# Attention of the first two sequences ahead of the layers, and each layer for both of them on one conversion of its weights

## The chip, the cores and the metric

The kernel runs on one core of one Trainium2 chip. The metric is the device time of one execution in microseconds (us). Three executions of the kernel before took 1094.45, 1095.03 and 1097.45 us; their median is 1095.03 us. About 0.3% (3.3 us) is what a comparison of runs of this kernel can tell from no change.

## The reference

Four sequences of 576 tokens go through attention with 8 heads of 64 channels, and then through two feed-forward layers (512 to 2048 to 512) with different activations. Scores further than `tau` below the row's largest one are left out of the softmax.

```python
scores = scale * np.matmul(q, k.transpose(0, 1, 3, 2))          # 4 x 8 x 576 x 576
thresh = np.max(scores, axis=-1, keepdims=True) - tau
scores = np.where(scores >= thresh, scores, -1000000000.0)
attn = softmax(scores);  x = (attn @ v), heads side by side      # 2304 x 512
h = x @ w_in;  g = h * np.clip(h + 3.0, 0.0, 6.0) / 6.0;  x = g @ w_out       # layer 1
h = x @ w_in2; r = np.maximum(h, 0.0); g = r * r;         out = g @ w_out2    # layer 2
```

The activations are float32, the four weight matrices float64.

## The kernel before, in words

**Attention.** A sequence is four units, each a pair of heads. A unit is nine jobs: four blocks of 128 queries of each head, and one job for the last 64 queries of both heads; a sequence is 36 jobs. A job computes its scores (L302 or L306) into one of three PSUM slots (tag `s`), takes their minimum on VectorE (L312; the queries carry a minus sign), the threshold (L314 on GpSimd or L316 on ScalarE), the exponential on ScalarE (L322), masks and sums on VectorE (L329, which is what gives the PSUM slot back), makes float16 and a remainder (`p16`: L335 on ScalarE, L336 and L337 on GpSimd), transposes them by a DMA (L339, tile `pt`), and five jobs later multiplies by the values (L361, tile `o`). `finish` transposes a unit's result back (`xT`) and copies it to `xr` (L392). The first sequence is "plain": one float32 product per half row, with the queries in the buffer of `ya` and `p16` in the weights' buffers `wpo`. The others split queries and keys into two parts, with four times as many products, each shorter, and with more work ahead of each unit (L230 to L244).

**Layers.** A hidden tile is 24 matmuls of 288 columns (L696, tile `hp`) for 128 of the 2048 hidden channels of one sequence, then ScalarE, VectorE, ScalarE and GpSimd (L700 to L707) make its two float16 parts. An output tile is 24 matmuls (L733, tile `y`), added to `ya` by L739. Both take PSUM slots of the same tag `s` as the scores. A layer of one sequence is 16 hidden and 16 output tiles, 32 tiles; a call of `moe` yields twice per tile.

**Weights.** A unit of weights (256 hidden channels, 1 MB of float64) is loaded (`wd`), its group's maximum taken (`group_scale`, L555), and it is converted on ScalarE, VectorE and GpSimd (L622 to L634) into two float16 parts in a buffer `wpi` or `wpo` (four of each), and stored to a scratch tensor (L636). There are 32 units, 16 of each layer. For the first sequence they are converted, for the others read back from the scratch: 96 reads of 512 KB.

**Order.** The eight blocks are layer 1 and 2 of sequence 1, layer 1 and 2 of sequence 2, and so on. The first sequence's attention runs alone but for two units of weights (`FIRST_W`, L846 on); the attention of the next one is fed in between the tiles of the current one by a count of steps (`attn_to` in the last loop). `tick` says at which tile a unit of weights is due: unit k at tile 2k - 8 but for the first few. At the end of layer 1 of each sequence the whole output's maximum sets the scale of layer 2's input (`all_max`, L130; `split_scaled`, L397, L398), which the next hidden tile needs; `BUBBLE` leaves attention steps for that place, and `keep_warm` puts idle matmuls there where none are left. The program is written in this order, and a scheduler with a model of time orders each engine's instructions by it, within what slots and data allow.

Of the kernel before, what the change touches and what calls it, by code (L numbers as in the profile page):

```python
# [29 lines left out]
SPLIT = 34  # L30
FIRST_DVE = 4
N_G, N_PT = 3, 7
NWD, N_W = 4, 4
LEAD = 8
BUBBLE = 8
WARM = (7, 6)
# [4 lines left out]
def attention_moe_moe_kernel(  # L41
# [55 lines left out]
    xr = [big.tile([P, S], F32, name=f"xr{c}") for c in range(NC)]  # L97
# [11 lines left out]
    q_pl = me.tile([P, 2, 2 * NT + 1, P], F32, name="ya", bufs=1)  # L109
    xh, xl = [None] * NC, [None] * NC  # L110
    xsc = {}

    def new_x(c):
        t = big.tile([P, 2, S], F16, tag=f"xh{c}", name=f"x16{c}")
        xh[c], xl[c] = t[:, 0], t[:, 1]

    last_vm = [None]

    def keep_warm(ins, n):

# [79 lines left out]
    def prep_steps(u):  # L200

        u.plain = u.b == 0
        if u.plain:

            u.qf = q_pl[:, u.i % 2]
            u.kf = xr[2 + u.i % 2]
# [102 lines left out]
    def soft1(j):  # L309
# [3 lines left out]
        if j.u.b == 0:  # L313
# [3 lines left out]
        if j.u.b == 0:  # L317
# [6 lines left out]
    def soft2(j):  # L324
# [5 lines left out]
        if u.b == 0:  # L330
# [43 lines left out]
    def finish(u, half):  # L374
# [8 lines left out]
        direct = u.b == 0 and u.p == NC - 1  # L383
        if direct and half == 0:
            new_x(u.p)
        for r, c, src in parts:
            if direct:
                s = xsc["s"]
                nc.scalar.activation(out=xh[u.p][r, c], in_=src, func=AF.Copy, scale=s[r])
                nc.vector.scalar_tensor_tensor(out=xl[u.p][r, c], in0=src, scalar=s[r], in1=xh[u.p][r, c], op0=ALU.mult, op1=ALU.subtract)  # L390
            else:
                nc.scalar.activation(out=xr[u.p][r, c], in_=src, func=AF.Copy)  # L392

    def split_scaled(src, s, cs=range(NC)):
        for c in cs:
            new_x(c)
            nc.scalar.activation(out=xh[c], in_=src[c], func=AF.Copy, scale=s)  # L397
            nc.vector.scalar_tensor_tensor(out=xl[c], in0=src[c], scalar=s, in1=xh[c], op0=ALU.mult, op1=ALU.subtract)  # L398

    def split_x(b, cs=range(NC)):  # L400
        s = xsc["s"] = st.tile([P, 1], F32, name="sx", bufs=2)
        e = st.tile([P, 1], F32, name="ex", bufs=2)
# [7 lines left out]
    def attention():  # L410
# [43 lines left out]
    def run(us, all_jobs, stop):  # L454
        n = len(all_jobs)
        pr = None
        for i in range(n + LAG):
# [438 lines left out]
```

## Time and profile before

| | |
|---|---|
| median of three executions | 1095.03 us |
| the profiled execution | 1099.09 us |
| its span, first to last instruction | 1097.2 us |
| TensorE busy | 1018.1 us, 93% |
| VectorE, ScalarE, GpSimd busy | 642.5, 654.2, 502.9 us |
| mean granted TensorE clock | 0.969 |

The profile is of one execution. "PE" is TensorE, "PEld" its weight loads, "DVE" VectorE, "ACT" ScalarE, "POOL" GpSimd and "SP" SyncE, which here only issues DMAs. An idle time in brackets names what ended it. The granted clock is a share of the full 2.4 GHz; the other level is half of that.

### The profile page before, as it was taken

How to read it: one execution, taken by the hardware profiler on the slowest of the kernel's cores; microseconds unless marked ns; L12 is line 12 of the kernel's file. 1: busy time of each engine (PE TensorE's matmuls, PEld its weight loads, DVE VectorE, ACT ScalarE, POOL GpSimd, SP SyncE). 2: the span in 40 equal slices, each digit the busy share in tenths (PEclk: the TensorE clock that was granted, in tenths of full speed). 3: DMA queues.
4: the chain of work that ended last, by engine and by line, in shares of the span. 5: the costliest groups of instructions: out<-in, count | busy, mean ns of one | idle time of the engine just before them, and what ended most of it. 6: DMA issues, size and time to landing. Idle time of an engine off the chain costs nothing.

```text
span 1097.2 us, 23339 instructions
## 1 busy us (share of the span) xinstructions
PE 1018.1 (93%) x9274; PEld 822.0 (75%) x9274; DVE 642.5 (59%) x1347; ACT 654.2 (60%) x1129; POOL 502.9 (46%) x629
## 2 busy tenths in 40 slices
PE   6877699797898999999999999999899999999998
PEld 4656476575776888888788888888788887778776
DVE  5886778879778885455855554555835231225122
ACT  5886798877887875655575465655654243223222
POOL 5876556754657664444354443344354212222111
PEclk9998699898998999999999999999999999999999
DMA  9999498988786786656565555555455342222211
GB/s 269 185 179 239 155 336 250 245 234 214 186 193 205 146 211 172 132 130 146 129 131 131 150 131 154 132 121 134 92 122 118 112 120 98 96 78 78 78 39 44
DMA packets 258765, 167.60 MB, mean 153 GB/s; under 512 B 215904, under 2 KB 228192, under 8 KB 258656
## 3 DMA queue, kind: packets, MB, share of 16 engines
q1 hardware_dynamic: 257008, 165.58, 60.2%
q8 instruction: 73, 1.20, 0.4%
q10 hardware_dynamic: 1648, 0.52, 0.2%
q14 instruction: 36, 0.29, 0.1%
HBM read 98.57 MB, written 21.50 MB: 109 GB/s over the span
## 4 chain that ended last, share of the span: by engine, by line
PE 70%; DVE 14%; DMA 7%; ACT 5%; issue 2%; POOL 1%; SPq 0%; ACTq 0%; POOLq 0%; DVEq 0%
PE y L733 30%; PE hp L696 29%; PE s L306 4%; PE o L361 3%; DMA wd<-in_moe_w_in_dram 3%; DVE wc L631 2%; DVE nm L312 2%; DVE e L329 2%; DMA pt<-wpo 1%; DMA wd<-in_moe_w_out_dram 1%; PE s L302 1%; DMA vraw<-in_v_dram 1%; DVE ya L739 1%; DVE g L555 1%; ACT e L322 1%
## 5 line engine op out<-in xcount | busy, mean ns | idle before, releaser
L696 PE MATMUL hp<-x,wpi 128*128 128x288 f16 x3072 | 403.9, 290 | 11.3 <-ACT wpi L633 5.0
L733 PEld LDWEIGHTS <-wpo 128*128 128x128 f16 x3072 | 298.3, 99 | 95.6 <-DVE e L329 8.9
L696 PEld LDWEIGHTS <-wpi 128*128 128x128 f16 x3072 | 299.2, 99 | 91.2 <-ACT wpi L633 5.3
L733 PE MATMUL y<-gh,wpo 128*128 128x288 f16 x2048 | 340.8, 290 | 17.3 <-DVE e L329 8.5
L707 POOL TENSOR_TENSOR gl<-g,gh 128x576 f16<-128x576 f32 x128 | 167.7, 1311 | 299.7 <-ACT gh L706 298.9
L733 PE MATMUL y<-gl,wpo 128*128 128x288 f16 x1024 | 210.9, 289 | 0.0
L312 DVE TENSOR_REDUCE nm<-s 128x1 f32<-128x576 f32 x144 | 107.7, 750 | 59.0 <-PE s L306 54.9
L739 DVE SCALAR_TENSOR_TENSOR ya<-y,yq,ya 128x576 f32<-128x576 f32 (+1 forms) x98 | 78.0, 802 | 98.3 <-PE y L733 98.0
L337 POOL TENSOR_TENSOR p<-e,p 128x512 f16<-128x512 f32 x108 | 127.2, 1178 | 0.0
L706 ACT ACTIVATE gh<-g 128x576 f16<-128x576 f32 x128 | 87.0, 680 | 55.1 <-DVE g L701 27.9
L329 DVE SCALAR_TENSOR_TENSOR e<-s,thr,e 128x576 f32<-128x576 f32 x108 | 87.9, 814 | 38.9 <-ACT e L322 37.9
L361 PE MATMUL o<-v,pt 128*128 128x64 f16 (+1 forms) x2016 | 90.0, 200 | 13.1 <-ACT os L368 6.7
L335 ACT ACTIVATE p<-e 128x576 f16<-128x576 f32 x108 | 73.6, 681 | 46.0 <-DVE e L329 39.8
L361 PEld LDWEIGHTS <-pt 128*128 128x128 f16 x2016 | 80.0, 100 | 24.9 <-issue 11.2
L306 PE MATMUL s<-k_st,q_st 128*128 128x288 f32 x480 | 94.3, 319 | 2.2 <-DVE g L701 1.2
L700 ACT ACTIVATE g<-hp,r_h,aq 128x576 f32<-128x576 f32 x64 | 52.9, 830 | 54.5 <-PE hp L696 54.4
L704 DVE TENSOR_TENSOR g<-g,hp 128x576 f32<-128x576 f32 x64 | 48.0, 749 | 63.6 <-ACT g L703 63.4
L701 DVE SCALAR_TENSOR_TENSOR g<-g,r_w,hp 128x576 f32<-128x576 f32 x64 | 51.8, 810 | 56.5 <-ACT g L700 56.3
L703 ACT ACTIVATE g<-hp,r_w 128x576 f32<-128x576 f32 x64 | 47.1, 735 | 56.4 <-PE hp L696 56.1
L322 ACT ACTIVATE e<-s,nm 128x576 f32<-128x576 f32 x108 | 78.5, 726 | 0.4
L336 POOL TENSOR_TENSOR p<-e,p 128x64 f16<-128x64 f32 x108 | 35.4, 327 | 91.6 <-issue 59.2
L344 POOL TENSOR_SCALAR sm<-sm,vsc 128x2 f32<-128x2 f32 (+1 forms) x80 | 23.0, 287 | 116.0 <-DVE e L329 102.0
(133 smaller groups left out, 1146.3 us busy)
## 6 DMA issues: line engine op xcount, KB each, us to landing
wpi<-scr SPq DMA_DIRECT2D x48, 512.0 KB, 3.5
wpo<-scr SPq DMA_DIRECT2D x48, 512.0 KB, 4.1
wd<-in_moe_w_in_dram SPq DMA_DIRECT2D x16, 1024.0 KB, 7.4
wd<-in_moe_w_out_dram SPq DMA_DIRECT2D x16, 1024.0 KB, 6.3
scr<-wpi SPq DMA_DIRECT2D x16, 512.0 KB, 7.0
scr<-wpo SPq DMA_DIRECT2D x16, 512.0 KB, 4.1
kraw<-in_k_dram SPq DMA_DIRECT2D x16, 256.0 KB, 4.4
vraw<-in_v_dram SPq DMA_DIRECT2D x16, 256.0 KB, 3.2
```

The lines of the kernel that those rows point to most:

```text
L306: nc.tensor.matmul(s[:, half, 0:HALF], lhsT=u.qs[sl][:, cs], rhs=u.ks[sl][:, kk, c], start=i == 0, stop=i == len(ops) - 1)
L312: nc.vector.tensor_reduce(out=j.nm, in_=j.s, axis=AX.XY, op=ALU.min)
L322: nc.scalar.activation(out=j.e, in_=j.s, func=AF.Exp, bias=j.nm, scale=-1.0)
L329: nc.vector.scalar_tensor_tensor(out=j.e, in0=j.s, scalar=j.thr, in1=j.e, op0=ALU.is_le, op1=ALU.mult, accum_out=u.sm[:, col:col + 1])
L335: nc.scalar.activation(out=p16[:, 0:S], in_=e, func=AF.Copy)
L337: nc.gpsimd.tensor_tensor(out=p16[:, S + TAIL:], in0=e[:, 0:NT * P], in1=p16[:, 0:NT * P], op=ALU.subtract)
L361: nc.tensor.matmul(o[:, n * w:n * w + w], lhsT=j.pt[:, c, :], rhs=vv[:, hs, vc, :], start=i == 0, stop=i == len(ops) - 1)
L696: last_hp[0] = nc.tensor.matmul(hp[:, a, 0:HALF], lhsT=wsl(tag, "i", f, w, c), rhs=x[c][:, a * HALF:(a + 1) * HALF], start=i == 0, stop=i ...
L706: nc.scalar.activation(out=gh, in_=gf, func=AF.Copy)
L707: nc.gpsimd.tensor_tensor(out=gl, in0=gf, in1=gh, op=ALU.subtract)
L733: mm = nc.tensor.matmul(a[:, k_, 0:HALF], lhsT=wsl(tag, "o", f, w, e), rhs=g[f][:, k_ * HALF:(k_ + 1) * HALF], start=i == 0, stop=i == len ...
L739: nc.vector.scalar_tensor_tensor(out=y, in0=av_, scalar=yq, in1=y, op0=ALU.mult, op1=ALU.add)
```

## The change

The attention of sequences 1 and 2 now comes first, all of it plain. Only then do the layers begin: layer 1 for sequences 1 and 2 in turn, a quarter of the hidden channels at a time (a "segment": four hidden and four output tiles), so that each unit of weights is converted once for both; then layer 2 for both in the same way; then layer 1 of sequence 3, layer 1 of sequence 4, layer 2 of sequence 3, layer 2 of sequence 4. A hidden tile of the next segment stands ahead of each segment's output tiles, also across a change of layer or sequence. The last eight jobs of sequence 2 are fed in beside the first four hidden tiles, sequence 3's attention up to tile 116 of 256, sequence 4's up to tile 150. Four units of weights are converted in the attention (after 50, 54, 58 and 62 steps); the other 28 are due one in every four tiles. Results of sequences 3 and 4 go through a scratch tensor in DRAM. Reads of converted weights fall from 96 to 64. `keep_warm` and `BUBBLE` are gone, as is the direct path from `xT` to the split input; the buffers of raw weights fall from four to three and those of `wc` from three to two.

```diff
-FIRST_W = (24, 30)
-FIRST_LD = 34
-FIRST_ATT = 15
+FIRST_W = (50, 54, 58, 62)
+FIRST_LD = 64
+AHEAD = 8
-EARLY = {2: 3, 3: 3, 4: 4, 5: 5, 6: 6, 7: 8}
+LEAD_J = 12
-NWD, N_W = 4, 4
-LEAD = 8
-BUBBLE = 8
-WARM = (7, 6)
+NWD, N_W = 3, 4
...
-        u.plain = u.b == 0
+        u.plain = u.b < 2
...
-            if direct:
-                s = xsc["s"]
-                nc.scalar.activation(out=xh[u.p][r, c], in_=src, func=AF.Copy, scale=s[r])
...
+            nc.scalar.activation(out=u.xr[r, c], in_=src, func=AF.Copy)
+        if half and not u.plain:
...
+            d = x_st[u.b][u.p] = scr.tile([P, S], F32, name=f"x_{u.b}{u.p}")
+            nc.sync.dma_start(out=d, in_=u.xr)
...
-    def plan(tag, layer, b, win, wout):
+    def plan(layer, bs, win, wout):
         def add(kind, u):
...
+            for b in bs:
+                wuse[(layer, b, kind, u)] = len(wseq)
+            wseq.append((win if kind == "i" else wout, kind, u, layer, bs[0]))
...
-        c = t = wt.tile([P, UW], F32, name="wc", bufs=3)
+        c = t = wt.tile([P, UW], F32, name="wc", bufs=2)
...
-            if EARLY.get(k, UC * k - LEAD) > step:
+            if (4 * k - LEAD_J if k < n_j else 4 * n_j + 2 * (k - n_j) - LEAD) > step:
                 break
...
+    blocks = [(1, (0, 1)), (2, (0, 1)), (1, (2,)), (1, (3,)), (2, (2,)), (2, (3,))]
...
+    jobs_b = 9 * NPAIR
+    a1 = 2 * jobs_b + LAG
+    a2 = a1 + PRE + jobs_b + LAG
+    a3 = a1 + PRE + 2 * jobs_b + LAG
+    split_x(0)
+    ways = [(0, a1 - AHEAD - LAG), (8, a1), (2 * 116, a2), (2 * 150, a3)]
+    done = {8: 1, 2 * 116: 2, 2 * 150: 3}
...
+    for i, g in enumerate(segs):
+        f0 = g.q * NQ
+        for f in range(f0 + (1 if i else 0), f0 + NQ):
+            go(hidden(g, f))
+        if i + 1 < len(segs):
+            go(hidden(segs[i + 1], segs[i + 1].q * NQ))
+        go(output(g))
```

What that does to the order stands below at two places. The first is ScalarE where the layers begin. Before (L700 and L706 are the first hidden tiles, L389 the last unit's result on its way into the layer, L230 the keys of sequence 2):

```order
L335 ACTIVATE wpo<-g 128x576 x2
L368 ACTIVATE os<-o,sm 128x64
L365 ACTIVATE os<-o,sm 64x64 x2
L368 ACTIVATE os<-o,sm 128x64 x2
L389 ACTIVATE x_1581<-xT,sx 128x256
L368 ACTIVATE os<-o,sm 128x64
L389 ACTIVATE x_1581<-xT,sx 64x64
L368 ACTIVATE os<-o,sm 128x64
L389 ACTIVATE x_1581<-xT,sx 64x64
L389 ACTIVATE x_1581<-xT,sx 128x256
L230 ACTIVATE k_st_94<-tps 64x256
```

The first L700 stands two rows on, when all 36 jobs are done. Now (line numbers of the changed file: L309 is the exponential, L322 makes `p16`, L355 and L352 scale an output, L378 copies a unit's result, L635 is the conversion of the fourth unit of weights, L706 the first hidden tile):

```order
L635 ACTIVATE wpo<-wc 128x1024
L309 ACTIVATE g<-s,nm 128x576
L355 ACTIVATE os<-o,sm 128x64
L322 ACTIVATE wpo<-g 128x576
L352 ACTIVATE os<-o,sm 64x64 x2
L355 ACTIVATE os<-o,sm 128x64
L322 ACTIVATE wpo<-g 128x576
L355 ACTIVATE os<-o,sm 128x64
L706 ACTIVATE g<-hp,r_h,aq 128x576
L378 ACTIVATE xr<-xT 128x256
L378 ACTIVATE xr<-xT 64x64 x2
L309 ACTIVATE g<-s,nm 128x576
```

Attention steps of sequence 2 stand on both sides of the first hidden tile. On TensorE the scores of 64 jobs and the products with the values of 56 stand ahead of the first hidden product, the other 8 and 16 behind it, the last of them between the output tiles of sequence 1's first segment.

The second place is VectorE at the first change from layer 1 to layer 2, from the scale's reduction of the `vm` product on. Before (L398 makes the inputs `x` of layer 2 from `ya`, L241 and L372 are attention, L670 and L720 small factors):

```order
L132 TENSOR_REDUCE mx<-vm 128x1
L137 TENSOR_SCALAR ex<-mx 128x1
L755 RECIPROCAL sx<-ex 128x1
L670 TENSOR_TENSOR e_3635<-ex 128x1
L720 TENSOR_SCALAR yq<-e_y_109,e_3635 128x1
L241 SCALAR_TENSOR_TENSOR q_st_92<-tps,qs,q_st_92 64x256
L398 SCALAR_TENSOR_TENSOR x_3528<-ya,sx,x_3528 128x576
L372 TENSOR_TENSOR os<-o,sm 128x2x64
L398 SCALAR_TENSOR_TENSOR x_3531<-ya,sx,x_3531 128x576
L398 SCALAR_TENSOR_TENSOR x_3534<-ya,sx,x_3534 128x576
L312 TENSOR_REDUCE nm<-s 128x1
L398 SCALAR_TENSOR_TENSOR x_3537<-ya,sx,x_3537 128x576
```

No layer tile (L701, L704 or L739) stands between. Now (L119, L124, L758 and L389 are the same chain; L707 is a hidden tile of sequence 2, still in layer 1; L633 and L557 belong to weights):

```order
L119 TENSOR_REDUCE mx<-vm 128x1
L633 SCALAR_TENSOR_TENSOR wc<-wc,wd 128x1024
L124 TENSOR_SCALAR ex<-mx 128x1
L633 SCALAR_TENSOR_TENSOR wc<-wc,wd 128x1024
L758 RECIPROCAL sx<-ex 128x1
L684 TENSOR_TENSOR e_5987<-ex 128x1
L299 TENSOR_REDUCE nm<-s 128x1
L707 SCALAR_TENSOR_TENSOR g<-g,r_w_102,hp 128x576
L359 TENSOR_TENSOR os<-o,sm 128x2x64
L730 TENSOR_SCALAR yq<-e_y_105,e_5987 128x1
L389 SCALAR_TENSOR_TENSOR x_5800<-ya,sx,x_5800 128x576
L557 TENSOR_REDUCE g_6188<-wd 128x1
```

Hidden tiles of the other sequence and weights stand inside the chain.

## Rows read from the trace of the kernel before

**Rows 1.** Stretches: length, busy us of each engine, granted clock, DMA share, GB/s.

```profile
core 0: us, PE busy (x) PEld busy (x) DVE busy (x) ACT busy (x) POOL busy (x), PEclk, DMA share, GB/s
0.00:97.80 97.80, 71.40 (x630) 53.33 (x630) 75.03 (x179) 76.91 (x158) 72.78 (x154) 0.95 1.05 225
97.80:264.70 166.90, 136.16 (x1117) 104.55 (x1115) 130.64 (x268) 129.90 (x191) 96.63 (x91) 0.89 0.83 232
264.70:542.30 277.60, 264.49 (x2560) 217.74 (x2560) 192.84 (x419) 190.87 (x341) 145.30 (x172) 0.97 0.69 170
542.30:784.30 242.00, 239.54 (x2290) 198.24 (x2291) 138.54 (x297) 143.07 (x265) 105.14 (x131) 0.99 0.56 132
993.90:1097.20 103.30, 98.66 (x804) 78.86 (x802) 27.08 (x43) 30.78 (x45) 20.42 (x16) 1.00 0.18 60
268.00:390.00 122.00, 111.91 (x1094) 91.47 (x1092) 98.41 (x221) 98.54 (x169) 76.63 (x84) 0.95 0.73 183
400.00:540.00 140.00, 139.98 (x1337) 115.76 (x1335) 82.81 (x165) 82.81 (x153) 60.05 (x76) 1.00 0.63 148
```

**Rows 2.** The same for L312 alone: (x) counts jobs.

```profile
35.30:75.50 40.20, 14.97 (x20) 1.00 1.08 188
75.50:98.80 23.30, 4.39 (x6) 0.85 1.16 262
97.80:264.70 166.90, 11.90 (x16) 0.89 0.83 232
264.70:542.30 277.60, 35.24 (x47) 0.97 0.69 170
542.30:784.30 242.00, 26.96 (x36) 0.99 0.56 132
268.00:390.00 122.00, 16.52 (x22) 0.95 0.73 183
400.00:540.00 140.00, 15.73 (x21) 1.00 0.63 148
```

**Rows 3.** The same for L622 alone: (x) counts units of weights.

```profile
97.80:264.70 166.90, 23.90 (x20) 0.89 0.83 232
268.00:390.00 122.00, 11.93 (x10) 0.95 0.73 183
```

**Rows 4.** TensorE in order of time: start, us, what [idle before <-releaser].

```profile
87.81 2.19 PE L302 MATMUL s<-xr,ya 128*128 128x288 f32 x8
...
276.30 0.98 PE L361 MATMUL o<-v,pt 128*128 128x64 f16 x28
...
334.04 0.65 PE L733 MATMUL y<-gh,wpo 128*128 128x288 f16 x4 [0.37 <-DVE e L329]
...
350.84 1.14 PE L733 MATMUL y<-gh,wpo 128*128 128x288 f16 x4 [5.02 <-DVE e L329]
...
1069.25 8.79 PEld L696 LDWEIGHTS <-wpi 128*128 128x128 f16 x72
```

**Rows 5.** Groups by form: count | busy us, mean ns | idle before, releasers.

```profile
L631 DVE SCALAR_TENSOR_TENSOR wc<-wc,wd 128x1024 int32<-128x1024 int32 x28 | 40.3, 1458 | 2.3 <-ACT wc L622 2.1
L555 DVE TENSOR_REDUCE g<-wd 128x1 f32<-128x1024 f32 x32 | 38.8, 1213 | 10.4 <-DMA wd<-in_moe_w_in_dram 8.1 <-DMA wd<-in_moe_w_out_dram 2.2
L622 ACT ACTIVATE wc<-wd,sp 128x1024 f32<-128x1024 f32 x32 | 38.2, 1233 | 1.9 <-DVE sp L561 1.8
L630 ACT ACTIVATE wd<-wd 128x1024 int32<-128x1024 uint16 x28 | 32.4, 1157 | 12.3 <-DMA wd<-in_moe_w_out_dram 7.8 <-DMA wd<-in_moe_w_in_dram 4.3
L633 ACT ACTIVATE wpi<-wc 128x1024 f16<-128x1024 f32 x16 | 16.7, 1055 | 3.1 <-DVE wc L631 2.4 <-DVE wc L626 0.7
L335 ACT ACTIVATE wpo<-g 128x576 f16<-128x576 f32 x36 | 24.4, 680 | 5.7 <-DMA pt<-wpo 4.6 <-DVE g L329 1.0
L337 POOL TENSOR_TENSOR wpo<-g,wpo 128x512 f16<-128x512 f32 x36 | 43.3, 1204 | 0.0
```

**Rows 6.** DMA issues from 35.3 to 75.5 us: count, median us to landing.

```profile
pt<-wpo SPq DMA_TRANSPOSE x20, 3.9
```

More of the change, by code (lines that the diff above doesn't have):

```diff
@@ L394, in split_scaled @@
[L394 to L402, printed above, removed]
+        if half == 0:
+            if u.plain:
+                if u.p == 0:
+                    x_st[u.b] = me.tile([P, NC, S], F32, tag="ya1", name="xr", bufs=1)
+                u.xr = x_st[u.b][:, u.p, :]
+            else:
+                u.xr = me.tile([P, S], F32, name="xr", bufs=2)
@@ L641, in w_next @@
         n = NQ // UC
+        if layer == 2 and kind == "i" and u % n == n - 1:
+            norm_scale(u // n)
         if k + 1 < min(len(wseq), most[0]) and wseq[k + 1][4] == 0 and wseq[k + 1][2] % n == 0:
             group_scale(k + 1)
-        if layer == 2 and kind == "i" and u % n == n - 1:
-            norm_scale(u // n)
     def want_w(k):
@@ L809, in moe @@
-        for qd in range(NG):
-            f0 = qd * NQ
-            for f in range(f0 + (1 if qd else 0), f0 + NQ):
-                yield from hidden(f)
-            if f0 + NQ < NF:
-                yield from hidden(f0 + NQ)
-            if qd == NG - 1 and before_last is not None:
-                before_last()
-            yield from output(qd)
-    blocks = [(f"{layer}_{b}", layer, b) for b in range(B) for layer in (1, 2)]
-    for tag, layer, b in blocks:
-        plan(tag, layer, b, *((moe_w_in, moe_w_out) if layer == 1 else (moe2_w_in, moe2_w_out)))
@@ L824, in attention_moe_moe_kernel, with write_last @@
-    need = {f"1_{b}": (b + 1) * 9 * NPAIR + (LAG + PRE if b else 0) for b in range(B)}
+        if last and layer == 2:
+            write(s, NC - 1)
+            yield
+            write(s, NC)
+            yield
+    def write_last(s, e):
+        ya, b = s.ya, s.b
+        n = TAIL if e == NC else P
+        ob = wt.tile([P, UW, 2], I32, name="wd", bufs=NWD).bitcast(F32).rearrange("p a b -> p (a b)")[:, 0:DM]
+        dst = out[b * S:b * S + NT * P, (NC - 1) * P:].rearrange("(p t) e -> p t e", t=NT)
+        for i0, i1 in ((0, 2), (2, 4)) if e < NC else ((0, 3), (3, 4)):
+            a = ps_a.tile([P, 512], F32, tag="acc", name="ot")
+            c = slice(i0 * P, i1 * P)
+            for i in range(i0, i1):
+                src = ya[:, i, NT * P:] if e == NC else ya[:, e, i * P:i * P + P]
+                nc.tensor.transpose(a[0:n, i * P:i * P + P], src, ident)
+            if e == NC:
+                nc.scalar.activation(out=ob[0:n, c], in_=a[0:n, c], func=AF.Copy)
+                continue
+            nc.vector.tensor_copy(out=ob[:, c], in_=a[:, c])
+            nc.sync.dma_start(out=dst[:, i0:i1], in_=ob[:, c].rearrange("p (t e) -> p t e", e=P))
+        if e == NC:
+            nc.scalar.dma_start(out=out[b * S + NT * P:(b + 1) * S, :], in_=ob[0:n])
@@ new lines, in write @@
+    def write(s, e):
+        ya, b = s.ya, s.b
+        if b == B - 1 and e >= NC - 1:
+            return write_last(s, e)
+        a = ps_a.tile([P, 512], F32, tag="acc", name="ot")
+        n = TAIL if e == NC else P
+        for i in range(4):
+            if e == NC:
+                nc.tensor.transpose(a[0:n, i * P:i * P + P], ya[:, i, NT * P:], ident)
+            else:
+                nc.tensor.transpose(a[:, i * P:i * P + P], ya[:, e, i * P:i * P + P], ident)
+        ob = wt.tile([P, UW, 2], I32, name="wd", bufs=NWD).bitcast(F32).rearrange("p a b -> p (a b)")[:, 0:DM]
+        if e == NC - 1:
+            nc.vector.tensor_copy(out=ob[0:n], in_=a[0:n])
+        else:
+            nc.scalar.activation(out=ob[0:n], in_=a[0:n], func=AF.Copy)
+        if e == NC:
+            nc.sync.dma_start(out=out[b * S + NT * P:(b + 1) * S, :], in_=ob[0:n])
+        else:
+            dst = out[b * S:b * S + NT * P, e * P:e * P + P].rearrange("(p t) e -> p t e", t=NT)
+            nc.sync.dma_start(out=dst, in_=ob.rearrange("p (t e) -> p t e", t=NT))
```

359 lines of the change are left out of this document (163 added, 196 removed).

## The prediction

> **What bounds the kernel now.** I read the stretches first [rows 1]. Between the ends that I chose lie the first sequence's attention (to 97.8 us, the first hidden product), layer 1 of sequence 1 (to 264.7), two blocks (to 542.3), two more (to 784.3), and, after a stretch not shown, the last block (from 993.9). The reader is to see that TensorE is full from about 400 us on (139.98 of 140 us between 400 and 540, clock 1.00) and not before. I call a stretch's lost time what PE stood idle plus what the clock took (length times one minus the granted clock). It is 30.7 + 18.4 = 49.1 us from 97.8 to 264.7, 13.1 + 8.3 = 21.4 to 542.3, 2.5 + 2.4 = 4.9 to 784.3. So some 75 us are lost after the first hidden product, nearly all of them while weights are converted (20 units to 264.7 and 10 more from 268 to 390, 30 of the 32) [rows 3].
>
> In the first 97.8 us no engine leads: VectorE has 75.0, ScalarE 76.9, GpSimd 72.8, TensorE 71.4 us, the DMA engines 1.05 [rows 1]. Undisturbed, 20 jobs take 40.2 us, 2.01 us each [rows 2]; the last six need 23.3 us, since two units of weights and three of the four conversions of x fall there.
>
> **The price of TensorE's work.** 72 weight loads in a row, one for each matmul, take 8.79 us [rows 4]: a tile of 24 is 2.93 us, a block of 32 is 93.8. The stretch to 784.3 has 239.5 - 2.4 = 237.1 us of work for 64 tiles (187.5) and 36 jobs [rows 2], so that a split sequence with its writing out costs 49.6 us, 1.38 a job. The stretch to 542.3 has 264.5 - 8.3 = 256.2 for 64 tiles and 47 jobs (64.8): 3.9 us are left for the small products of ten units, 0.4 each.
>
> **The change part by part.**
>
> First, the attention of sequence 2 moves from between the tiles, where TensorE was not the only bound, to a place with no tiles. By the order, 64 jobs stand ahead of the first hidden product. Of the first sequence's 36 jobs, 20 start between 35.3 and 75.5 and six later, so the 31st starts at 75.5 [rows 2]. Jobs 31 to 64 add 34 x 2.01 = 68.3 us: 143.8. On top come four units of weights and the split of x. Before, two units and three quarters of the split made six jobs 23.3 - 12.1 = 11.2 us longer; twice that, 22.4, is the upper bound. The lower one is ScalarE's own part, 4 x (1.23 + 1.06) + 3 = 12 us [rows 5] (the 3 is an estimate for four copies of 576 columns at the rate of L335). I take 20, near the upper one, since every engine is full there: the first hidden product at **164 us**, with 156 to 172 as bounds. That sequence 2 is plain now is in the 2.01: scores of 2.19 / 2 = 1.10 us a job (four of the eight records of rows 4), less work ahead of each unit.
>
> Second, TensorE's work from there on: 256 tiles, 750.1; two split sequences, 99.2; what is left of sequence 2, 8 scores (8.8), 16 products with the values at 0.98 / 2 = 0.49 (7.8; 28 matmuls are two jobs) [rows 4] and some transposes (2.4, estimated), 19; small products for 28 units, 11; the end as it is, 103.3 - 93.8 = 9.5 [rows 1] less some 1.5 for the change of layer in it, 8. Sum: **887 us**, give or take 8.
>
> Third, the lost time, on which the answer hangs. I take it by stage.
>
> (a) The last eight jobs. Their chain (exponential, mask, `p16`, transpose, values, `finish`, split) has to end before the first hidden tile of sequence 2 can. TensorE has four tiles of sequence 1, most of a fifth, and outputs to put beside. I take 6 us (2 to 14).
>
> (b) The joint layers up to tile 116, 112 tiles beside the 36 jobs of sequence 3: 328 + 49.6 + 7 = 385 us of work with 28 conversions, one in 13.7 us. Before, 268 to 390 us had ten conversions [rows 3] and 22 jobs in 122 us and lost 10.1 + 6.1 = 16.2 us, 13.3%; 400 to 540 had none and 21 jobs, and lost nothing [rows 1, 2]. Busy shares there: DVE and ACT 81% against 59%. In the new stage DVE has 138.5 us as in the stretch to 784.3, 48 more tiles at 27.08 / 32 = 0.85, and 28 x (1.21 + 1.46) [rows 1, 5]: 254 us, 66%. ACT has 143.1 + 48 x 0.96 + 28 x (1.23 + 1.16 + 1.06) = 286, 74%. Between the two stretches of before, a straight line gives 4.2% by DVE (16 us) and 9.1% by ACT (35). The long waits of TensorE were for DVE's L329 [rows 4], so I stay nearer to the first: 22 us.
>
> (c) Tiles 116 to 150 with all 36 jobs of sequence 4: 34 x 2.93 + 49.6 = 149 us, DVE 138.5 - 30 x 0.85 = 113, 76%. The line gives 10%, 15 us; but no conversions stand ahead of L329 there, so I take half, 8.
>
> (d) The changes of layer: by the order, hidden tiles of the other sequence stand in the chain that TensorE had waited for, and the same holds for sequences 3 and 4. I cost them at nothing; if that cover fails, it is a few us each, as in the 4.9 of the stretch to 784.3, which holds one such change.
>
> Lost in all: 6 + 22 + 8 = **36 us** (10 to 75). The rest I cost at nothing. The 16 DMAs by which sequences 3 and 4 go through DRAM have 24 half tiles until they are needed, some 35 us. The 32 reads of weights that go were beside a full TensorE. One raw buffer less is covered by conversions that come less than half as often as before (28 in 385 us, against ten in 122); where it isn't, it is part of (b).
>
> Sum: 164 + 887 + 36 = 1087 us of span. The profiled execution took 1099.1 us with a span of 1097.2, so 1.9 us lie around it: 1089. That is 10 us less than 1099.1; the median of the runs is 1095.0, 4 us below the profiled one, so I predict **1085 us**.
>
> **Rivals.**
>
> Nothing is lost in the joint layers: conversions come rarely enough that they look like 400 to 540. Lost 10 instead of 36: 1059. For it speaks that DVE needs 0.85 of a tile's 2.93 us for the tile itself; against it, that ACT is at 74%.
>
> Slower: the joint layers keep the waits of 268 to 390. There a tile of TensorE waited 5.02 us for L329, the instruction that gives a PSUM slot back, and its next four matmuls took 1.14 instead of 0.65 us [rows 4]: a job's slot is held while DVE is behind with weights, in order. At 13.3% of 385 this is 51 us, with 15 for (c) and 6 for (a) 72 us: 1121. It decides against the change from 46 us of lost time on. For it speaks that every conversion has the same five large instructions as before and the raw loads have one buffer less, when L555 already waited 10.4 us for them [rows 5]; against, the longer distance between conversions.
> The Trainium skill (Trainium Kernel Development and Optimization, Best Practices) says that regular bubbles can mean that SBUF or PSUM has run out. By that rule the three slots, which the change leaves, are the limit, and this rival gains; that the wait's releaser is L329 agrees, and that 21 jobs in 140 us lost nothing with the same three slots does not.
>
> The attention of sequence 2 gets dearer than that of sequence 1. Two of the four `wpo` buffers hold weights while the last 15 jobs still write `p16` into them. A buffer is taken for at least 0.68 + 1.20 + 3.9 = 5.8 us [rows 5, 6], so with two of them a job takes 2.9 us: 15 x 0.9 = 13 us, 1098. For it speaks the order; against, that eight of the 15 have tiles beside them.
>
> TensorE falls to its lower clock in the longer attention. Its busy time there is 71.4 / 36 = 1.98 us a job; at the lower level, by 1.14 / 0.65, it would be 3.5 and the bound: 64 x 1.5 = 95 us more, 1180. But the granted clock was 1.00 from 35.3 to 75.5 us [rows 2], with these same jobs.
> The Trainium skill (TensorE: Matmul & The Clock Gate, Part 1: The HAM clock gate) has the half rate as the default, released by sustained activity and back after idleness, which would speak against a long stretch of scattered small matmuls; this trace's 1.00 there does not bear it out.
>
> That the change doesn't do what it says is ruled out by the order.
>
> **How the numbers follow.** My forecast (1072 to 1098, its own range) 0.46; nothing lost 0.19; slower by the joint layers 0.19; dearer attention 0.13; clock 0.03. A measurement tells 0.3%, 3.3 us, from no change. Faster than 1091.7: 0.38 of the forecast's share, all of the second, 0.03 of the fourth: 0.60. Within 0.3%: 0.06 + 0.06 + 0.01 (from the third) = 0.13. Slower: 0.02 + 0.18 + 0.04 + 0.03 = 0.27. The range, 1062 to 1112, leaves out about half of the second and of the third case and the last.
>
> **What would show it.** The first hidden product between 156 and 172 us; 2.0 us a job up to the 50th; TensorE's idle plus clock loss of about 36 us behind it, most of it in the some 400 us that follow; no wait of over 2 us around the products for the scale of layer 2's input; a full TensorE from about 760 us on. I am wrong if the first hidden product comes after 175 us, if the joint layers lose over 46 us with L329 or an L555 waiting for its load as releaser, or if the stage of sequence 4's attention takes much over 160 us.

## The result and the profile after

The changed kernel takes 1103.31 us, the median of nine executions (1098.41 to 1104.51); nine of the kernel before took 1095.66 (1094.45 to 1098.73). The ratio is 1.0056, with a 95% interval of 1.0038 to 1.0074. The change made the kernel slower by 0.6%, where 0.9% faster was forecast (1085 against 1095.03). The profiled execution has a span of 1101.5 us (1097.2 before).

The stretches of the changed kernel, with the columns of [rows 1]. The ends are the first hidden product (171.4), the last product with sequence 2's values (215), and round figures; the last row reaches to the end.

```profile
0.00:171.40 171.40, 130.06 (x1170) 96.33 (x1171) 132.73 (x321) 141.87 (x297) 126.06 (x260) 0.92 1.00 203
171.40:215.00 43.60, 35.78 (x397) 27.68 (x396) 23.06 (x44) 29.89 (x59) 27.58 (x44) 1.00 0.67 129
215.00:300.00 85.00, 78.36 (x643) 61.86 (x641) 62.33 (x134) 70.15 (x100) 45.56 (x38) 0.99 0.69 208
300.00:420.00 120.00, 114.99 (x1053) 93.63 (x1051) 79.69 (x158) 74.10 (x117) 60.42 (x64) 1.00 0.51 139
420.00:725.00 305.00, 292.61 (x2808) 240.92 (x2806) 199.27 (x435) 204.71 (x360) 154.87 (x179) 0.99 0.59 144
725.00:1101.00 376.00, 372.21 (x3172) 299.81 (x3169) 121.74 (x197) 125.81 (x190) 89.46 (x83) 1.00 0.32 95
```

The exchange was nearly even. Before, the first hidden product came at 97.8 us and 999.4 us lay behind it; now it comes at 171.4, 73.6 us later, and 930.1 lie behind it, 69.3 fewer. The difference, 4.3 us, is that of the two spans. TensorE's idle time behind the first hidden product fell from 52.7 us (999.4 less 946.7 busy) to 36.1, and its granted clock there rose from 0.97 to 0.99. The forecast had 66.2 us later and 76.4 fewer: the attention ahead of the layers took 7.4 us more than that, and the layers gave back 7.1 less.

The jobs by stretch, counted at their minimum (L299 now, L312 in [rows 2]):

```profile
35.30:75.50 40.20, 15.14 (x21) 1.00 1.06 187
75.50:92.50 17.00, 3.46 (x6) 0.81 0.91 181
92.50:140.00 47.50, 16.45 (x22) 1.00 0.99 169
140.00:171.40 31.40, 4.49 (x6) 0.73 0.95 255
```

Undisturbed a job takes 1.91 us (40.2 / 21) and, later, 2.16 with two units of weights in the stretch. Six jobs take 17 us where sequence 2 begins, and the last six 31.4 us, with two more units and at a granted clock of 0.73. The 17 us hold no conversion; what makes them long stays open.

Two things in this trace were not in the forecast. The first is how the eight last jobs end. This is the chain of work that ended last, from 173.7 to 208 us (start, us, what), with pieces left out:

```profile
173.74 4.96 DMA pt<-wpo
178.72 0.44 ACT wpo L322
...
179.84 1.13 POOL wpo L324
180.98 3.46 DMA pt<-wpo
...
188.66 3.77 DMA pt<-wpo
...
192.84 3.18 DMA pt<-wpo
196.05 0.69 ACT wpo L322
...
197.17 1.11 POOL wpo L324
198.31 3.19 DMA pt<-wpo
201.58 0.69 ACT wpo L322
...
202.70 1.12 POOL wpo L324
203.85 3.97 DMA pt<-wpo
```

The reader is to see one ring: ScalarE writes `p16`, GpSimd adds the remainder, the DMA transposes it, and only when the transpose has landed does ScalarE write again. Two of the four `wpo` buffers hold weights, and the jobs go round the other two. From 178.7 to 207.9 us each of the two is written again after 5.5 to 6.9 us, which makes a job every 2.7 us (11 in 29.2 us). TensorE idles 7.8 us in the stretch from 171.4 to 215 (43.6 less 35.78), 4.9 of it in waits for these transposes:

```profile
PE o L348 <- DMA pt<-wpo: 4.9, 5, 1.5
```

(us in total, times, longest.)

The second is when weights are converted. The forecast spread 28 units evenly over the joint layers, one in 13.7 us. These are the first steps on ScalarE, two units each (start, us, instruction), of the changed kernel:

```profile
219.92 2.37 ACT L624 ACTIVATE wc<-wd,sp 128x1024 f32<-128x1024 f32 x2
234.90 2.42 ACT L624 ACTIVATE wc<-wd,sp 128x1024 f32<-128x1024 f32 x2
253.80 2.39 ACT L624 ACTIVATE wc<-wd,sp 128x1024 f32<-128x1024 f32 x2
272.98 2.38 ACT L624 ACTIVATE wc<-wd,sp 128x1024 f32<-128x1024 f32 x2
290.58 2.37 ACT L624 ACTIVATE wc<-wd,sp 128x1024 f32<-128x1024 f32 x2
335.45 2.38 ACT L624 ACTIVATE wc<-wd,sp 128x1024 f32<-128x1024 f32 x2
```

Five pairs begin within 71 us, 15 to 19 us apart, and then none for 45. That is one unit in 8.8 us at first (four gaps of two units in 70.7 us), denser than the one in 12.2 of the kernel before from 268 to 390 us [rows 3]. The order of the instructions showed it: the pairs stand behind 4, 7, 9, 13, 14, 21, 25, 30, ... hidden tiles, where the count of steps asks for one pair in eight tiles, that is, in four hidden ones. The scheduler had drawn them forward.

### The profile page after: what moved, and what is told of

It reads as the page before. It is cut to its first block, busy times and chain, and to the rows that moved or that the text cites. A ratio compares the mean times of both kernels' runs of the same rounds, so it can differ in the third digit from the quotient of the medians.

```text
span 1101.5 us, 23226 instructions
## 1 busy us (share of the span) xinstructions
PE 1024.0 (93%) x9232; PEld 820.2 (74%) x9232; DVE 618.8 (56%) x1286; ACT 646.5 (59%) x1118; POOL 503.9 (46%) x665
## 4 chain that ended last, share of the span: by engine, by line
PE 58%; DMA 14%; DVE 11%; ACT 8%; issue 4%; POOL 4%; SPq 0%; POOLq 0%; ACTq 0%; DVEq 0%
PE y L742 27%; PE hp L702 22%; DMA wd<-in_moe_w_in_dram 4%; DMA wd<-in_moe_w_out_dram 3%; DMA vraw<-in_v_dram 3%; PE o L348 2%; DVE wc L633 2%; PE s L293 2%; DMA pt<-wpo 2%; PE s L289 2%; ACT wc L624 1%; ACT wpo L322 1%; DVE nm L299 1%; POOL wpo L324 1%; ACT g L309 1%
## 5 line engine op out<-in xcount | busy, mean ns | idle before, releaser
L702 PE MATMUL hp<-x,wpi 128*128 128x288 f16 x3072 | 396.2, 287 | 8.3 <-DVE g L707 2.5
L742 PE MATMUL y<-gh,wpo 128*128 128x288 f16 x2048 | 334.1, 286 | 8.3 <-DVE g L710 3.3
L742 PE MATMUL y<-gl,wpo 128*128 128x288 f16 x1024 | 207.3, 286 | 0.3 <-POOL gl L713 0.3
L299 DVE TENSOR_REDUCE nm<-s 128x1 f32<-128x576 f32 x144 | 107.7, 750 | 25.0 <-PE s L293 16.3
L289 PE MATMUL s<-kf,q_pl 128*128 128x288 f32 x288 | 94.2, 457 | 17.4 <-DVE g L316 14.1
L348 PEld LDWEIGHTS <-pt 128*128 128x128 f16 x2016 | 79.2, 99 | 31.4 <-issue 13.2
L706 ACT ACTIVATE g<-hp,r_h,aq 128x576 f32<-128x576 f32 x64 | 52.8, 826 | 62.4 <-PE hp L702 60.6
L707 DVE SCALAR_TENSOR_TENSOR g<-g,r_w,hp 128x576 f32<-128x576 f32 x64 | 51.8, 810 | 60.3 <-ACT g L706 60.1
L324 POOL TENSOR_TENSOR p<-e,p 128x512 f16<-128x512 f32 x72 | 84.5, 1173 | 0.0
L324 POOL TENSOR_TENSOR wpo<-g,wpo 128x512 f16<-128x512 f32 x72 | 84.0, 1166 | 0.0
L289 PEld LDWEIGHTS s<-kf,q_pl 128*128 128x128 f32 x288 | 54.7, 209 | 32.7 <-issue 11.3
L316 DVE SCALAR_TENSOR_TENSOR e<-s,thr,e 128x576 f32<-128x576 f32 x72 | 58.5, 815 | 27.3 <-ACT e L309 26.0
L322 ACT ACTIVATE p<-e 128x576 f16<-128x576 f32 x72 | 49.0, 680 | 34.7 <-DVE e L316 23.6
L316 DVE SCALAR_TENSOR_TENSOR g<-s,thr,g 128x576 f32<-128x576 f32 x72 | 58.0, 810 | 15.6 <-ACT g L309 12.8
```

What stands on the lines that cost most here:

```text
L289: nc.tensor.matmul(s[:, half, 0:HALF], lhsT=u.qf[:, t, :], rhs=u.kf[:, c], start=True, stop=True)
L299: nc.vector.tensor_reduce(out=j.nm, in_=j.s, axis=AX.XY, op=ALU.min)
L316: nc.vector.scalar_tensor_tensor(out=j.e, in0=j.s, scalar=j.thr, in1=j.e, op0=ALU.is_le, op1=ALU.mult, accum_out=u.sm[:, col:col + 1])
L322: nc.scalar.activation(out=p16[:, 0:S], in_=e, func=AF.Copy)
L324: nc.gpsimd.tensor_tensor(out=p16[:, S + TAIL:], in0=e[:, 0:NT * P], in1=p16[:, 0:NT * P], op=ALU.subtract)
L348: nc.tensor.matmul(o[:, n * w:n * w + w], lhsT=j.pt[:, c, :], rhs=vv[:, hs, vc, :], start=i == 0, stop=i == len(ops) - 1)
```

## The experiments

Every ratio is to runs of the kernel before that were taken with it; the interval is the 95% one. "First product" is the first hidden product in the profiled execution.

| kernel | median us | ratio | interval | first product |
|---|---|---|---|---|
| changed kernel | 1103.3 | 1.0056 | 1.0038 to 1.0074 | 171.4 |
| p16_own | 1092.2 | 0.9965 | 0.9943 to 0.9987 | 165.5 |
| outunits_late | 1100.0 | 1.0027 | 1.0014 to 1.0040 | 163.5 |
| loads_early | 1100.0 | 1.0036 | 1.0016 to 1.0056 | 172.2 |
| one_seq_per_layer | 1111.1 | 1.0151 | 1.0105 to 1.0197 | 169.0 |
| p16_all | 1096.3 | 0.9989 | 0.9973 to 1.0005 | 170.2 |
| p16_own_one_seq | 1105.2 | 1.0073 | 1.0048 to 1.0098 | 167.2 |
| p16_own_ahead16 | 1092.6 | 0.9963 | 0.9948 to 0.9977 | 152.1 |
| p16_own_out_late | 1098.4 | 1.0023 | 1.0003 to 1.0042 | 162.8 |
| maximum_late | 1087.4 | 0.9928 | 0.9910 to 0.9945 | 170.9 |
| p16_own_maximum_late | 1078.9 | 0.9863 | 0.9840 to 0.9886 | 163.7 |
| before_three_raw | 1109.9 | 1.0135 | 1.0120 to 1.0150 | |
| p16_own_maximum_late_ahead16 | 1085.7 | 0.9900 | 0.9871 to 0.9928 | 149.3 |
| before_maximum_late | 1103.9 | 1.0059 | 1.0039 to 1.0079 | |
| p16_own_maximum_late_one_seq | 1105.5 | 1.0077 | 1.0050 to 1.0103 | 165.7 |
| p16_own_maximum_late_loads | 1080.7 | 0.9851 | 0.9826 to 0.9877 | 166.1 |
| p16_own_maximum_late_ahead4 | 1080.9 | 0.9851 | 0.9826 to 0.9877 | 176.3 |
| even_conversions | 1084.8 | 0.9898 | 0.9875 to 0.9921 | 170.7 |
| p16_own_even_conversions | 1077.8 | 0.9842 | 0.9810 to 0.9874 | 165.2 |

**The buffers of `p16`.** The theory: two buffers are too few for the last jobs; the rival: every engine is full there anyway.

```diff
-            p16 = new_w("o").rearrange("p a b -> p (a b)")[:, 0:2 * S]
+            if u.b == 1 and j.n % 2:
+                p16 = at.tile([P, 2 * S], F16, name="p16")
+            else:
+                p16 = new_w("o").rearrange("p a b -> p (a b)")[:, 0:2 * S]
```

> Every second job of sequence 2 writes its float16 pair p16 into the two buffers that the split sequences use, instead of into the weights' buffers. Theory A (the last jobs of sequence 2 go round two free buffers of wpo: in the changed kernel's chain 0.69 us to write, 1.13 on GpSimd, 3.2 to 5.0 for the transposing DMA, again and again from 173.7 to 208 us): the stretch from the first hidden product to the last product with sequence 2's values gets shorter by most of the 7.8 us that TensorE idles there, and the jobs 55 to 64 ahead of it by a few; total 1092 to 1098 us against 1103. Theory B (every engine is near full there, a buffer more only moves the wait): within 3 us of 1103.

It took 0.9% (1.0056 less 0.9965; 10 us) off the changed kernel. This is the stretch from 171.4 to 215 us of p16_own:

```profile
171.40:215.00 43.60, 41.18 (x487) 33.69 (x486) 22.94 (x58) 30.96 (x65) 24.08 (x39) 1.00 0.59 113
```

TensorE idles 2.4 us in it instead of 7.8, and the first product comes 5.9 us earlier. The same length behind p16_own's own first product:

```profile
165.50:209.10 43.60, 39.83 (x469) 32.20 (x469) 24.77 (x56) 33.47 (x70) 29.70 (x49) 1.00 0.74 152
```

Counted so, TensorE idles 3.8 us instead of 7.8. Theory A holds in the total and in the idle time. The stretch to the last product with sequence 2's values did not get shorter, as it had it (some 44 us in both, to 215.3 and to 209.5), but more layer work is done in it: by 215 us 213 layer matmuls have begun instead of 146. The same two buffers bring 0.7% (7 us) on top of maximum_late and 0.6% (6 us) on top of even_conversions, two kernels that follow, and a first product 7.2 and 5.5 us earlier. The Trainium skill (Perfetto Trace Analysis, Optimization Strategy) says that a gap that repeats on the engine that should be saturated can mean too few buffers for the next tile. The forecast had weighed that rule for the PSUM slots alone. The runs agree with it for a ring in SBUF: two more buffers took 4.0 us of the gaps away (7.8 less 3.8), with the three PSUM slots unchanged.

> As p16_own, and for sequence 1 too: every second job of both plain sequences writes p16 into the split sequences' two buffers, six buffers in all instead of four. Theory A (with four free buffers, as sequence 1 has, nothing waits for one: a buffer is taken some 6 us and a job starts every 1.9): the same as p16_own, 1090 to 1094. Theory B (the transposes' landing holds up sequence 1 too): the 31 jobs to 75.5 us come 3 us or more earlier, 1086 to 1089.

The `u.b == 1` of the diff is left out. Six buffers for sequence 1 too brought nothing more: 0.2% slower than p16_own if anything, outside both expectations, and the first product came at 170.2 us although the ring is gone here as well. From 140 to 171 us its conversions waited for raw loads instead, two of 8.05 and 9.51 us on the chain, and TensorE worked only 16.87 us of 31 there. Why the loads came later is open.

**The attention ahead of the first tile.** Two edits move work out of it, one the loads in it.

```diff
-FIRST_W = (50, 54, 58, 62)
+FIRST_W = (54, 58)                  # outunits_late; units 2 and 3 due at tiles 1 and 2
...
-LOADS = (2, 4, 6)
+LOADS = (1, 2, 3)                   # loads_early
-AHEAD = 8
+AHEAD = 16                          # or 4; FIRST_W and FIRST_LD moved by the same 8 (or 4)
```

> Only two units of weights are converted ahead of the first hidden tile; the two for the output tiles come behind it, in the first and second hidden tile's place. Theory A (ahead of the first hidden tile all engines are full, a unit costs there what ScalarE and VectorE need for it, 3.5 us, while beside the tiles it is hidden): first hidden product at about 164 instead of 171.4 us, total 1096 to 1099. Theory B (the conversions were filling waits of the attention, or come back as a wait of the first output tiles): within 3 us of 1103.

> The loads of a unit two ahead are issued after jobs 1, 2 and 3 of a unit instead of after 2, 4 and 6. Theory A (at the change from sequence 1 to 2, 75 to 92 us with 6 jobs in 17 us, loads that SyncE issues behind transposes come late: the changed kernel's chain has a 3.7 us load of vraw at 78.6 and one of 3.4 at 119.5, and TensorE waits 6.4 us for kraw in all): first hidden product 4 to 6 us earlier, total 1097 to 1099. Theory B (that stretch is long because copies, the split of x for sequence 1 and the tails fall together; the load is only what came last): within 2 us of 1103.

> p16_own, with the two units for the output tiles converted behind the first hidden tile as in outunits_late. Theory A (part of outunits_late's 3 us was the two wpo buffers that stayed free longer, and p16_own has that already): within 2 us of p16_own, 1090 to 1094. Theory B (the two gains are separate: conversions ahead of the first tile cost time of their own): 1087 to 1090.

> p16_own, with 16 jobs of sequence 2 instead of eight beside the first four hidden tiles. Theory A (a job ahead of the tiles costs 2 us in which TensorE works 1.5; beside tiles its rest is covered): first hidden product 14 to 17 us earlier, of which TensorE's own work, 8 jobs at some 1.5, comes back, so 3 to 6 us gained: 1086 to 1089. Theory B (four tiles are too little to put beside 16 jobs; the chain of the last jobs sets when sequence 2 can be split): 1091 to 1096.

outunits_late brought the first product 7.9 us forward and kept some 3 of it, between the two theories. On top of p16_own it cost 6 us: neither theory. From 171 to 215 us TensorE then worked 36.40 us of 44 instead of 41.58, with two conversions there. loads_early moved nothing that can be told from the changed kernel (the intervals overlap, the first product is no earlier). With 16 jobs behind it the first product comes 13.5 us earlier than in p16_own and the time is the same. So when the first product comes is no measure of the time: what is taken from ahead of it comes back behind it.

**Sharing the conversions.**

```diff
-    blocks = [(1, (0, 1)), (2, (0, 1)), (1, (2,)), (1, (3,)), (2, (2,)), (2, (3,))]
+    blocks = [(1, (0,)), (1, (1,)), (2, (0,)), (2, (1,)), (1, (2,)), (1, (3,)), (2, (2,)), (2, (3,))]
...
-            if (4 * k - LEAD_J if k < n_j else 4 * n_j + 2 * (k - n_j) - LEAD) > step:
+            if max(1, 2 * k - LEAD) > step:
```

> Both attentions come first as in the changed kernel, but each layer is done for sequence 1 and then for sequence 2 with the weights read back, so a unit of weights is due every two tiles in sequence 1's layers instead of every four. Theory A (spreading the conversions is what the change gains: the kernel before lost 49 us with 20 units in 167 us and the changed one loses some 20 between 213 and 620): 20 to 40 us are lost again, total 1125 to 1145. Theory B (conversions are no trouble once sequence 2's attention is out of the tiles' way, so the sharing is worth little): 1103 to 1112.

> p16_own, with each layer done for sequence 1 and then for sequence 2 (weights read back, conversions twice as dense). Theory A (one_seq_per_layer cost only 8 us more than the changed kernel since its first four units all go to wpi, so that the wpo buffers stayed free for p16; the sharing itself is worth some 19 us): 1107 to 1113 against 1092 for p16_own. Theory B (sharing conversions is worth some 8 us): 1097 to 1103.

Undoing the sharing costs 1.0% (1.0151 less 1.0056; 10 us) in the changed kernel and 1.1% (12 us) with p16_own. The first lies in theory B's range, at its upper end, and far under theory A's; the second lies between the two theories. The first four units also change with it: all go to `wpi`, so one_seq_per_layer has no ring of two buffers, and the comparison with p16_own is the cleaner one. Theory A had rested on the 49 us that the kernel before lost beside 20 units in 167 us; the next runs bear on why so little of that came back.

**The wait or the spacing.** VectorE stood 30.8 us at L557 for raw loads (10.4 at L555 before, [rows 5]), so maximum_late holds that reduction back.

```diff
-        if k + 1 < min(len(wseq), most[0]) and wseq[k + 1][4] == 0 and wseq[k + 1][2] % n == 0:
+        if k + 1 < len(FIRST_W) and wseq[k + 1][4] == 0 and wseq[k + 1][2] % n == 0:
             group_scale(k + 1)
...
             if due > step:
+                if due - 1 <= step and wseq[k][4] == 0 and wseq[k][2] % (NQ // UC) == 0:
+                    with tc.issue_after(last_dv[0].ins):     # a layer tile's last VectorE instruction
+                        group_scale(k)
                 break
```

> The changed kernel, with the maximum over a group of weights (the reduction of the raw load on VectorE) held behind a layer tile's VectorE work shortly ahead of its conversion, instead of as soon as the conversion before it is done. Theory A (with three raw buffers the load of a group's second unit starts only when a conversion has given its buffer back, and the reduction stands ahead of everything on VectorE until it has landed: 30.8 us in the changed kernel against 10.4 before, 4.4 of them just ahead of the first hidden product): the wait falls under 5 us, first hidden product 4 us earlier, total 1094 to 1099. Theory B (VectorE has slack beside the tiles, so most of the 30.8 costs nothing, and the conversions come later for it): 1101 to 1106.

> p16_own and maximum_late together. Theory A (two separate losses): 1083 to 1088, 4 to 9 us under p16_own. Theory B (the reduction's wait is hidden behind TensorE's queue of tiles): within 3 us of p16_own, 1089 to 1095.

1.3% (14 us) and, on top of p16_own, 1.0% (11 us): the largest step so far, more than either theory A had. VectorE's wait is gone, but part of it went to ScalarE, which waits for raw loads at L632 (L633 in maximum_late). The groups (count | busy us, mean ns | idle before, releasers), first two of the changed kernel and of maximum_late on ScalarE, then maximum_late's maximum:

```profile
L632 ACT ACTIVATE wd<-wd 128x1024 int32<-128x1024 uint16 x28 | 32.7, 1167 | 21.5 <-DMA wd<-in_moe_w_in_dram 10.8 <-DMA wd<-in_moe_w_out_dram 10.4
L633 ACT ACTIVATE wd<-wd 128x1024 int32<-128x1024 uint16 x28 | 31.9, 1140 | 33.3 <-DMA wd<-in_moe_w_out_dram 16.3 <-DMA wd<-in_moe_w_in_dram 15.8 <-DVE sm L332 1.1
L557 DVE TENSOR_REDUCE g<-wd 128x1 f32<-128x1024 f32 x32 | 37.7, 1211 | 0.0
```

The first product did not come earlier, as theory A had it (170.9 against 171.4). Of the next three runs, which ask whether the wait is the cause, one speaks for it and two against.

> The kernel before with three raw buffers of weights instead of four, as the change leaves them. Theory A (the fourth buffer is what let loads land ahead of the reduction): VectorE's wait for loads rises from 10 us to over 25 and the kernel gets 5 to 15 us slower, 1100 to 1110. Theory B (loads are covered either way): within 3 us of 1096.

> The kernel before with the same hold of the weights' maximum behind a tile's VectorE work. Theory A (with four raw buffers and a wait of 10.4 us in all the loss is small, and it is the change's three buffers that made it 30.8): 1090 to 1098 against 1095. Theory B (the hold is worth the same 16 us in the kernel before): 1078 to 1084, and the change would bring nothing.

> p16_own_maximum_late with each layer done for sequence 1 and then for sequence 2, conversions twice as dense, weights read back. Theory A (sharing keeps its worth of 10 to 12 us, as one_seq_per_layer and p16_own_one_seq showed): 1089 to 1092 against 1079. Theory B (what sharing brought was mostly fewer waits of VectorE for raw loads, which the hold takes away already): 1079 to 1084.

Three raw buffers take VectorE's wait in the kernel before from 10.4 to 22.7 us and make it 1.4% slower. But the hold, which takes that wait from 10.4 to 2.0 us, makes it 0.6% slower as well, and with layers done one sequence at a time it takes the wait from 37.5 to 11.8 us and brings nothing; both came out slower than either of their theories. So a shorter wait alone decides nothing. maximum_late had also spaced the pairs evenly, behind 4, 9, 13, 17, 21, ... hidden tiles. even_conversions does that and leaves the maximum early:

```diff
+        first = k >= len(FIRST_W) and u % (NQ // UC) == 0
+        with tc.issue_after(last_ac[0].ins) if first else nullcontext():   # a hidden tile's first ScalarE step
-        nc.scalar.activation(out=c, in_=d[:, :, 1].bitcast(F32), func=AF.Prelu, scale=sp, alpha=2.0 ** 32)
+            nc.scalar.activation(out=c, in_=d[:, :, 1].bitcast(F32), func=AF.Prelu, scale=sp, alpha=2.0 ** 32)
...
```

> The changed kernel with the first conversion of each pair of units held on ScalarE behind a hidden tile's work, every fourth hidden tile, and the maximum left as early as it was. Theory A (the wait of VectorE for raw loads is the loss): the wait stays at some 30 us or grows, total 1100 to 1108. Theory B (the bunched conversions were the loss, the wait only stood beside it): about maximum_late's time, 1085 to 1091, with VectorE's wait for loads still there.

> p16_own and even_conversions together. Theory A (the wait is the loss): near p16_own, 1089 to 1096. Theory B (the spacing is): near p16_own_maximum_late, 1077 to 1083.

1.6% (17 us) and 1.2% (13 us). The groups of L557 (count | busy us, mean ns | idle before, releasers), first of the changed kernel:

```profile
L557 DVE TENSOR_REDUCE g<-wd 128x1 f32<-128x1024 f32 x32 | 38.9, 1217 | 30.8 <-DMA wd<-in_moe_w_in_dram 17.9 <-DMA wd<-in_moe_w_out_dram 12.8
```

and of even_conversions:

```profile
L557 DVE TENSOR_REDUCE g<-wd 128x1 f32<-128x1024 f32 x32 | 39.0, 1218 | 25.5 <-DMA wd<-in_moe_w_in_dram 13.0 <-DMA wd<-in_moe_w_out_dram 12.4
```

Most of the wait is still there and the time is gone: theory B, the spacing. Two edits that space the pairs, one through VectorE and one through ScalarE, end with overlapping intervals. Not separated is where in a tile a pair stands, which the hold sets too. Nor is it shown that VectorE's wait costs nothing while conversions are bunched; one run, with one sequence at a time, shows no gain from shortening it there. The pairs of even_conversions on ScalarE:

```profile
218.90 2.39 ACT L627 ACTIVATE wc<-wd,sp 128x1024 f32<-128x1024 f32 x2
236.21 2.39 ACT L627 ACTIVATE wc<-wd,sp 128x1024 f32<-128x1024 f32 x2
264.02 2.38 ACT L627 ACTIVATE wc<-wd,sp 128x1024 f32<-128x1024 f32 x2
290.33 2.41 ACT L627 ACTIVATE wc<-wd,sp 128x1024 f32<-128x1024 f32 x2
317.74 2.40 ACT L627 ACTIVATE wc<-wd,sp 128x1024 f32<-128x1024 f32 x2
345.31 2.39 ACT L627 ACTIVATE wc<-wd,sp 128x1024 f32<-128x1024 f32 x2
```

and its stretches:

```profile
171.40:215.00 43.60, 37.09 (x413) 28.96 (x412) 22.11 (x44) 29.20 (x59) 27.56 (x44) 0.98 0.63 120
215.00:300.00 85.00, 82.02 (x663) 65.82 (x662) 56.22 (x123) 66.50 (x98) 41.68 (x38) 1.00 0.58 173
300.00:420.00 120.00, 118.51 (x1108) 97.00 (x1106) 90.30 (x183) 82.01 (x127) 67.39 (x70) 1.00 0.62 168
420.00:725.00 305.00, 299.09 (x2927) 248.36 (x2925) 202.12 (x444) 213.16 (x375) 159.08 (x187) 0.99 0.61 152
725.00:1101.00 376.00, 352.31 (x2961) 282.96 (x2957) 111.72 (x175) 112.37 (x165) 80.05 (x68) 1.00 0.28 87
```

From 236 us on the pairs stand 26 to 30 us apart. TensorE's idle time from 215 to 725 us falls from 24.0 to 10.4 us, spread over all three rows; that is 13.7 of the 19.9 us by which the span is shorter. What went are waits for VectorE: 19.3 us of TensorE's idle time there ended with one of its instructions in the changed kernel, 7.7 in even_conversions. With the sharing undone the hold cannot space pairs that are due every four tiles, which fits that run; that is argued, not shown. With the pairs spaced, sharing is worth 2.1% (1.0077 less 0.9863; 23 us) instead of 1.0%.

> p16_own, maximum_late and 16 jobs instead of eight beside the first four hidden tiles. p16_own_ahead16 brought the first hidden product 13.5 us forward and gained nothing in all. Theory A (the last eight jobs' chain takes the time that four tiles and eight jobs more need, whatever VectorE waits for): within 2 us of p16_own_maximum_late. Theory B (VectorE's wait for loads is what the 16 jobs met): 3 to 6 us faster than it.

> p16_own_maximum_late with the attention's loads issued after jobs 1, 2, 3 of a unit. Theory A (loads_early gained 2 to 3 us over the changed kernel, and that is a third, separate loss): 1075 to 1077. Theory B (that was chance or another order): within 3 us of 1079.

> p16_own_maximum_late with four jobs of sequence 2 beside the first four hidden tiles instead of eight (16 cost some 7 us). Theory A (each of these jobs ahead of the tiles costs 2 us in which TensorE works 1.5): 1080 to 1083. Theory B (the jobs beside the first tiles cost as much there as ahead of them): within 2 us of 1079. Theory C (the last jobs' chain, which holds up the split of sequence 2, is what matters, and fewer jobs behind the first tile shorten it): 1074 to 1077.

Four jobs or eight, and the loads, make no difference; 16 cost 0.4% (the intervals just overlap, 4 us by the ratios), against both theories: the last product with sequence 2's values then comes at 212.1 instead of 207.6 us, so that the 16 jobs end later, not earlier. The lowest time is that of p16_own_even_conversions, 1.6% under the kernel before and 2.1% under the changed one; p16_own_maximum_late's interval overlaps it.

## Why the prediction was wrong

The direction was wrong; the time lay inside the range. The forecast of 1085 was 18.3 us too low, in three parts: 7.4 us up to the first hidden product, 7.1 behind it (930.1 against 887 + 36 = 923), and 4 that were taken off because the profiled execution of before lay above its median; the changed kernel's did not. The gain forecast was 10 us, so overruns of this size were enough to turn it round.

**The first step failed by its size: 171.4 us, not 164.** It lies inside the bounds of 156 to 172, at their upper end. The term that failed is what comes on top of the 34 jobs at 2.01 us, put at 20: measured it is 27.6 (171.4 - 75.5 - 68.3), above the 22.4 that the forecast itself called the upper bound; with that bound the sum would have ended at 166.2, not 172. In p16_own the same term is 21.7 (165.5 - 143.8): the last six jobs take 25.5 us there instead of 31.4. "That sequence 2 is plain now is in the 2.01" was wrong, since 2.01 us a job was measured with four buffers for `p16`. This is the third rival (two of four `wpo` buffers hold weights), which got 0.13. It priced the loss at 13 us, from 2.9 us a job; the ring gave a job every 2.7 us, and p16_own shows 10, 5.9 of them ahead of the first product (6 and 7 us in the two kernels with even conversions). That p16_all has its first product at 170.2 us without the ring stays open. "Against, that eight of the 15 have tiles beside them" was no argument: the ring held those eight up too.

**The second step, TensorE's work, and terms (a) and (c) held.** Busy time behind the first product is 894.0 us, of which the clock took 6: 888 of work against 887. The eight last jobs lost 7.8 us against 6 (2 to 14). Tiles 116 to 150 (626 to 780 us) lost 8.5, of which 6.8 idle, against 8.

**Term (b) had the right size by luck.** Its 22 us rested on one conversion in 13.7 us, and on VectorE's busy share between two stretches of before. Up to tile 116 (215 to 626 us) 20.6 were lost, 17.2 idle and 3.4 by the clock. But the conversions came in bunches, one in 8.8 us at first, and these bunches, not the busy share, were most of the loss: with even spacing the same tiles (215 to 605.6 us) lost 4.5. even_conversions has the spacing that the forecast assumed: there (b) by itself is near the rival "nothing is lost", and the kernel is 1.0% faster than before. That its 1084.8 us meet the forecast of 1085 is luck too: a first product 7 us late and a (b) 17 us too high cancel in part. The order of the changed kernel was at hand and showed the bunches; the forecast took the count of steps for the place. Since the sizes agreed, the sum was not hurt by it.

**"One raw buffer less is covered" had a wrong reason, and what it cost stays open.** The reason, conversions "less than half as often as before", does not follow from its own numbers: 28 in 385 us is one in 13.7, ten in 122 one in 12.2, only a tenth less often. The buffer was not covered: VectorE's wait trebled and ScalarE's at L632 rose from 12.3 us (L630 before, [rows 5]) to 21.5, but even_conversions keeps 25.5 of the 30.8 us and is 1.6% faster than the changed kernel all the same, while the kernel before got 1.4% slower with three. The changed kernel with four was not tried; beside its other buffers there is no room for four.

**The second rival did not come**: no wait of 5 us for a slot; the longest of TensorE's waits from 215 to 725 us is 3.3. (d), put at nothing, nearly held: TensorE waited 3.7 us in all for the inputs x (L388, L389), never over 1.3 at a time. A granted clock under 1.00 in the attention is seen from 75.5 to 92.5 us (0.81, TensorE idle 28% of the time) and from 140 to 171 (0.73, idle 40%), not where jobs run undisturbed. Of the signs, 2.0 us a job up to the 50th did not come (six jobs took 17 us, the next 22 took 2.16 each). None of the conditions named for being wrong was met: they asked for one large miss, and the margin of 10 us was smaller than the sum of small overruns on one side.

## What to carry to other kernels

A buffer that two stages share must be counted at the hand-over: how long one is held, divided by how many are left, is the least time per job, to be set against the time that is wanted. Where a scheduler orders the program, read from its order where periodic work really stands before spreading its cost evenly; even spacing was worth 1.6% here. And an idle engine in order is only a loss if somebody waits: look for who, and test it, as even_conversions did, before the wait gets the blame.

## What the runs showed of the hardware

In the changed kernel a transposing DMA of 128 by 1152 float16 landed 3.2 to 8.1 us after its issue (3.5 by the median; 3.2 to 4.0 from 181 to 208 us), so a ring of two buffers gave one job in 2.7 us, though its busy steps are 0.7, 0.3 and 1.1 us. A raw load of 1 MB took 6.2 us by the median, from 4.8 to 10.0. In even_conversions VectorE stood 25.5 us, in order, for such loads, in a kernel that was faster than the one before.
